# The last rows of a decode kernel's output product, and which engine waits for the output store

## The chip, the cores and the metric

The kernel runs on one core of a Trainium2 chip. The metric is the device time of one execution in microseconds. The core has a matrix engine (TensorE, "PE" in the profile; its weight loads are "PEld"), a vector engine (VectorE, "DVE"), a scalar engine (ScalarE, "ACT"), GpSimd ("POOL") and SyncE ("SP"), which here issues nearly all DMAs. Sixteen DMA engines carry the transfers.

## The reference

One token is decoded. Its normalised vector goes through an attention over a long cache and, beside it, through a small MLP block; all is summed.

```python
xn = layernorm(A_x)                                    # 1 x 1 x 1024
q  = (xn @ wq)                                         # 32 heads of 128
s  = einsum(q, repeat(k_cache, 8)) * 128 ** -0.5       # 4 KV heads x 65536 x 128
o  = einsum(softmax(s), repeat(v_cache, 8)) @ wo       # 4096 x 1024
h  = shift(gelu(layernorm(xn) @ w1)) @ w2              # 1024 x 1024 each
x1 = xn + h
h2 = gelu(layernorm(x1) @ w3) @ w4                     # 1024 x 3584, 3584 x 1024
return A_x + o + x1 + h2                               # bf16
```

All inputs are bf16. The two caches hold 64 MiB (67 MB) each, and each byte is used once.

## The kernel before

The program is written engine by engine. A planner in the file (`_Q`, `_B`, `_op`, `_grp`, `_dma`) keeps one list of operations for each engine and puts a semaphore wait in front of an operation where a buffer it reads or writes is still in use. `q_sp`, `q_pool` and the others are these lists; `wait_all` puts a bare wait at the present end of a list (L37; in the trace such a wait carries line L73).

All loads go through SP's queue in a fixed order: wq, w1, w2, w3, then blocks of 32,768 cache rows of K and V in turn, wo, and at last w4. A large SBUF tile `KV` with three slots takes them. The block loop runs over eight blocks, two for each KV head; TensorE's part of it is a hardware loop. In a block VectorE transposes the K block in place (`Ttr`, L460), TensorE forms scores (`QK`, L474), ScalarE exponentiates, and TensorE multiplies by V (`PV`, L518).

After the last block comes the tail, to which the change belongs:

- `resid_rows` (L598) adds the residual `acc` into one PSUM row for each half of the 1024 outputs, and `wo_rows` (L605) adds the attention's product with wo, 64 matmuls of 512 columns. VectorE (L611) and ScalarE (L612) copy the two rows to SBUF, and four matmuls (L614) put them into bank 0 of the PSUM tile `S_ps` as four rows of 256, on partitions 0, 32, 64 and 96.
- w4 stays as 28 row groups ("rows" below) of 1024 columns; TensorE multiplies row r by column r of `gh_bf`, in four column strips at once. The loads of w4 are cut as `w4_parts` (L569): rows 0 to 16, rows 17 to 23, rows 24 to 26, and row 27 in two halves. They are issued back to back on SP, in front of the end of the last block.
- `out_rows` (L584) takes parts 0 and 1 into bank 0. VectorE copies that bank to SBUF (`ost`, L677).
- `out_halves` (L591) takes rows 24 to 27 in half-width products of 128 columns into banks 2 and 3, one for each half of a strip. For the second half of row 27 `kept_matmul` (L561) uses the weights that TensorE still holds. VectorE adds each bank to its part of `ost` and writes bf16 to `orow` (L682).
- SP issues the store of `orow` (L684) and, as the last instruction of the program, waits for it (L685).

To make the halves, the columns of every strip are ordered as "h j n" (half, strip, column) instead of plainly, in `w4_row`, `resid_rows`, `wo_rows` and in the store.

Of the kernel before, what the change touches and what calls it, by code (L numbers as in the profile page):

```python
# [6 lines left out]
BF = mybir.dt.bfloat16  # L7
F32 = mybir.dt.float32
ACTF = mybir.ActivationFunctionType
ALU = mybir.AluOpType  # L10
# [106 lines left out]
def _op(q, fn, reads=(), writes=(), partial=False, loop=False):  # L117
    _deps(q, reads, writes)
    ev = q.op(fn, True, loop)
    _done(ev, reads, writes, partial)  # L120
    return ev


def _grp(q, fns, reads=(), writes=(), partial=False):
    _deps(q, reads, writes)
    ev = None
    for i, fn in enumerate(fns):
        ev = q.op(fn, i == len(fns) - 1)
    _done(ev, reads, writes, partial)
    return ev  # L130
# [8 lines left out]
def _dma(q, chan, fn, reads=(), writes=(), partial=False):  # L139
    _deps(q, reads, writes)  # L140
    chan.n += 1
    ev = q.dma(fn, chan.sem, 16 * chan.n)
    _done(ev, reads, writes, partial)
    return ev


def bass_parallel_sum__gqa_block_cached__mixer_s_mlp__decode_kernel(
# [13 lines left out]
    P = 128  # L161
    D = A_x.shape[2]
# [6 lines left out]
    KT_F = F // P  # L169
# [9 lines left out]
    with ExitStack() as es:  # L179
        E = es.enter_context  # L180

        def sb(name, shape, dt):
            return E(nc.sbuf_tensor(name, shape, dt))
# [7 lines left out]
        ident_f = sb("ident_f", [P, P], F32)  # L191
# [9 lines left out]
        pT_f = sb("pT_f", [P, 2, 512], F32)  # L201
# [8 lines left out]
        o_bf = sb("o_bf", [P, 32], BF)  # L210
        acc = sb("acc", [P, KT_D], F32)
        gh_bf = sb("gh_bf", [P, KT_F], BF)
# [3 lines left out]
        KV = sb("KV", [P, 3, SLOT], BF)  # L216
# [1 line left out]
        cb_W = sb("cb_W", [P, 4, G, 4], F32)  # L218
        cb_R = sb("cb_R", [P, P], F32)
        cb_o = sb("cb_o", [P, 32], F32)  # L220
        orow = sb("orow", [P, 2, 128], BF)

        e_off = [8 * F]

# [36 lines left out]
        S_ps = ps("S_ps", [P, 4, 512], F32)  # L261
# [12 lines left out]
        def chan(name):  # L274
            if name not in chans:
                chans[name] = _DmaChan(sem("d_" + name))
            return chans[name]
# [14 lines left out]
        def rows_src(w, r0, nrow):  # L292
            return w.rearrange("(p r) n -> p (r n)", p=P)[:, r0 * w.shape[1]:(r0 + nrow) * w.shape[1]]
# [81 lines left out]
        fns = []  # L375
# [173 lines left out]
            _op(q_dve, lambda e: e.reduce_sum(cb_o[0:32, :], cb_R[0:32, :].rearrange("p (a j) -> p j a", j=32), axis=AX.X), reads=[b_cb], writes=[b_cb])  # L549
            _op(q_dve, lambda e: e.tensor_copy(o_bf[32 * h:32 * h + 32, :], cb_o[0:32, :]), reads=[b_cb], writes=[b_o], partial=True)  # L550

        def weights_of(i):
            return (i.tile_position, i.tile_size, str(i.ins[1].memref), i.ins[1].offset, str(i.ins[1].ap))

        def keep_weights(i, name=""):
            r = mybir.InstMatmult(name=name or i.name, engine=i.engine, ins=list(i.ins), outs=list(i.outs), debug=i.debug, start_tensor_calc=i.start_tensor_calc,
                                  stop_tensor_calc=i.stop_tensor_calc, tile_size=i.tile_size, tile_position=i.tile_position,
                                  bass_skip_group_check=i.bass_skip_group_check, ldweights=False)
            return r

        def kept_matmul(e, out_, lhs, rhs, pos):  # L561
            i = e.matmul(out_, lhs, rhs, start=False, stop=True, tile_position=pos, skip_group_check=True).ins
            body = nc.m.functions[0].blocks[-1].instructions
            at = max(k for k, j in enumerate(body) if j.name == i.name)
            assert body[at].opcode == "Matmult" and any(j.opcode == "Matmult" and weights_of(j) == weights_of(i) for j in body[at - 6:at])
            del body[at]
            return e.add_instruction(keep_weights(i, "I-%d" % (1000000 + int(i.name[2:]))))

        w4_parts = [(0, 17 * D), (17 * D, 24 * D), (24 * D, 27 * D), (27 * D, 27 * D + 512), (27 * D + 512, 28 * D)]  # L569
        b_W4 = [_B() for _ in w4_parts]  # L570

        def w4_dma(i):
            c0, c1 = w4_parts[i]
            _dma(q_sp, chan("w4%d" % i), lambda e: e.dma_start(out=KV[:, 2, c0:c1], in_=rows_src(B_w4, 0, KT_F)[:, c0:c1]), writes=[b_W4[i]])

        n_bulk = 2
        b_half = [b_S[2], b_S[3]]
        ost = pT_f[:, 1, 0:256]
        b_ost = b_pT[1]

        def w4_row(r, jj):
            return KV[:, 2, r * D:(r + 1) * D].rearrange("p (h j n) -> p j h n", h=2, j=4)[:, jj, :, :]

        def out_rows(i):  # L584
            c0, c1 = w4_parts[i]
            _grp(q_pe, [lambda e, r=r, jj=jj: e.matmul(
                S_ps[32 * jj:32 * jj + 1, 0, 0:256].rearrange("p (h n) -> p h n", h=2), gh_bf[:, r:r + 1], w4_row(r, jj),
                start=False, stop=(i == n_bulk - 1), tile_position=(0, 32 * jj), skip_group_check=True) for r in range(c0 // D, c1 // D) for jj in range(4)],
                reads=[b_W4[i], b_gh], writes=[b_S[0]], partial=True)

        def out_halves(r, halves, i, first=False, last=False):  # L591
            def mm(e, hf, jj):
                f = kept_matmul if halves == (1,) else lambda e, *a: e.matmul(*a[:3], start=first, stop=last, tile_position=a[3], skip_group_check=True)
                return f(e, S_ps[32 * jj:32 * jj + 1, 2 + hf, 0:128], gh_bf[:, r:r + 1], w4_row(r, jj)[:, hf, :], (0, 32 * jj))
            _grp(q_pe, [lambda e, hf=hf, jj=jj: mm(e, hf, jj) for hf in halves for jj in range(4)],
                 reads=[b_W4[i], b_gh], writes=[b_half[hf] for hf in halves], partial=not first)

        def resid_rows():  # L598
            idc = ident_f[:, :].rearrange("p (h j n) -> p j h n", h=2, j=2)
            _grp(q_pe, [lambda e, j=j, jj=jj: e.matmul(  # L600
                S_ps[32 * jj:32 * jj + 1, 1, :].rearrange("p (h n e) -> p h n e", h=2, e=8)[:, :, :, j], acc[:, j:j + 1], idc[:, jj, :, :],
                start=(j == 0), stop=False, tile_position=(0, 32 * jj), skip_group_check=True) for j in range(KT_D) for jj in range(2)],
                reads=[b_acc, b_const], writes=[b_S[1]])

        def wo_rows():  # L605
            _grp(q_pe, [lambda e, j=j, jj=jj: e.matmul(  # L606
                S_ps[32 * jj:32 * jj + 1, 1, :].rearrange("p (h n) -> p h n", h=2), o_bf[:, j:j + 1],
                KV[:, 0, j * D:(j + 1) * D].rearrange("p (h j n) -> p j h n", h=2, j=2)[:, jj, :, :],
                start=False, stop=(j == 31), tile_position=(0, 32 * jj), skip_group_check=True) for j in range(32) for jj in range(2)],
                reads=b_KV[0] + [b_o], writes=[b_S[1]], partial=True)  # L610
            _op(q_dve, lambda e: e.tensor_copy(pT_f[0:1, 0, :], S_ps[0:1, 1, :]), reads=[b_S[1]], writes=[b_pT[0]])  # L611
            _op(q_act, lambda e: e.activation(pT_f[32:33, 0, :], S_ps[32:33, 1, :], ACTF.Copy), reads=[b_S[1], b_pT[0]], writes=[b_pT[1]])  # L612
            src = pT_f[0:64, 0, :].rearrange("p (h j n) -> p j h n", h=2, j=2)
            _grp(q_pe, [lambda e, jj=jj: e.matmul(  # L614
                S_ps[32 * jj:32 * jj + 1, 0, 0:256].rearrange("p (h n) -> p h n", h=2), ident_f[0:64, 32 * (jj // 2):32 * (jj // 2) + 1], src[:, jj % 2, :, :],
                start=True, stop=False, tile_position=(0, 32 * jj), skip_group_check=True) for jj in range(4)],
                reads=[b_pT[0], b_pT[1], b_const], writes=[b_S[0]])

        def loop_sync(h):
            if h > 0:  # L620
# [51 lines left out]
        _op(q_pool, lambda e: e.memset(pT_f[0:64, 0, :], 0.0), writes=[b_pT[0]])  # L672
        resid_rows()
        wo_rows()
        for i in range(n_bulk):
            out_rows(i)
        _op(q_dve, lambda e: e.tensor_copy(ost, S_ps[:, 0, 0:256]), reads=[b_S[0]], writes=[b_ost])  # L677
        for r in range(24, 27):
            out_halves(r, (0, 1), 2, first=(r == 24))
        for hf in range(2):  # L680
            out_halves(27, (hf,), 3 + hf, last=True)
            _op(q_dve, lambda e, hf=hf: e.tensor_tensor(out=orow[:, hf, :], in0=ost[:, 128 * hf:128 * hf + 128], in1=S_ps[:, 2 + hf, 0:128], op=ALU.add),  # L682
                reads=[b_ost, b_half[hf]], writes=[b_orow], partial=(hf == 1))
        ev_out = _dma(q_sp, chan("out"), lambda e: e.dma_start(out=out[0, 0, :].rearrange("(h j n) -> j h n", h=2, j=4), in_=orow[0:97:32, :, :]), reads=[b_orow])  # L684
        q_sp.wait_all([ev_out])  # L685

        code = nc.m.functions[0].blocks[0].instructions
        heads = {e: next(i for i in code if i.opcode == "Drain" and i.engine == e) for e in (nc.sync.engine, nc.scalar.engine)}
# [51 lines left out]
        for k, i in enumerate(code):  # L740
            if i.opcode != "Matmult":
                continue
            key = weights_of(i)
            if key == prev and i.ins[1].dtype == BF and not i.sync_info:
                code[k] = keep_weights(i)
                n_ld += 1
            prev = key
        assert n_ld > 40, n_ld
# [28 lines left out]
```

## Time and profile before

| What | Value |
|---|---|
| Median of 4 runs | 400.35 us (400.27 to 400.57) |
| The profiled execution's own time | 400.40 us |
| Its span, first to last instruction | 399.1 us |
| Mean granted TensorE clock | 0.645 |
| DMA packets | 3907, 169.97 MB, 426 GB/s over the span |
| Last w4 loads, issue to landing | 28 to 33 us |
| Store of the output | 2.0 KB, issue instruction 0.68 us |

The span begins with the first instruction of the kernel and ends with the last; the time of an execution also holds what the runtime puts around them. Lines of the profile read "line engine operation out<-in shape xcount | busy". An idle time in brackets names what ended it. "SPq" is SP's instruction stream, where DMAs are issued.

### The profile page before, as it was taken

The page shows a single profiled execution, that of the slowest core. Times are in us where ns is not written, and L with a number is a line of the kernel's source. Part 1 is how long each engine was busy: PE and PEld are TensorE (multiplying, and loading weights), DVE is VectorE, ACT ScalarE, POOL GpSimd, SP SyncE. Part 2 cuts the span into 40 slices and gives each one's busy share as a digit, 9 for nine tenths or more (in the row PEclk, how much of TensorE's full clock was granted, in tenths as well). Part 3 has the DMA queues.
Part 4 walks back from the last instruction along what each step waited for, and adds up shares of the span by engine and source line. Part 5 has one row for each costly group of instructions (what it writes and reads, how often), then busy time and mean ns, then how long its engine had stood idle before and what let it go on. Part 6 is the DMA issues. An engine that isn't in the chain of part 4 may idle for free.

```text
span 399.1 us, 3462 instructions
## 1 busy us (share of the span) xinstructions
PE 169.1 (42%) x1539; PEld 59.2 (15%) x1496; DVE 221.9 (56%) x262; ACT 23.9 (6%) x50; POOL 7.6 (2%) x31
## 2 busy tenths in 40 slices
PE   0034767338033713460357036413541362137394
PEld 0011334012001200110012011100120110012232
DVE  0024222994298549834984597269647952895201
ACT  1000000011001100110011002000100110011000
POOL 5000000000000000000000000000000000000000
PEclk9998568555655665575557555855585558555969
DMA  9999899999999999999999999999999999999995
GB/s 421 421 388 493 383 428 466 460 416 427 420 434 422 420 453 466 420 427 420 427 434 420 447 466 427 421 420 427 434 427 447 466 427 420 420 427 434 418 413 231
DMA packets 3907, 169.97 MB, mean 426 GB/s; under 512 B 572, under 2 KB 828, under 8 KB 956
## 3 DMA queue, kind: packets, MB, share of 16 engines
q1 hardware_dynamic: 3756, 169.87, 98.7%
q8 instruction: 5, 0.08, 0.1%
q10 hardware_dynamic: 144, 0.00, 0.0%
q14 instruction: 2, 0.02, 0.0%
HBM read 169.87 MB, written 0.00 MB: 426 GB/s over the span
## 4 chain that ended last, share of the span: by engine, by line
DMA 59%; DVE 25%; PE 13%; issue 1%; ACT 1%; SPq 0%; POOL 0%; DVEq 0%
DMA KV<-in_A_k_cache_dram 45%; DVE KV L460 18%; DMA KV<-in_B_w_dram 8%; DMA KV<-in_A_x_dram 6%; PE S_ps L411 3%; PE OT_ps L518 2%; DVE mrow L481 2%; PE M_ps L426 2%; PE S_ps L474 2%; PE S_ps L379 1%; ACT p_sb L496 1%; DVE Yall L395 1%; DVE pT_f L509 1%; DVE pT_f L419 1%; PE PT_ps L505 0%
## 5 line engine op out<-in xcount | busy, mean ns | idle before, releaser
L460 DVE STREAM_TRANSPOSE KV<-KV 128x4096 f32<-128x4096 f32 x32 | 140.3, 4421 | 44.3 <-DMA KV<-in_A_k_cache_dram 44.3
L474 PE MATMUL S_ps<-KV,Ycur 128*32 128x512 bf16 x512 | 60.7, 624 | 132.5 <-DVE KV L460 132.5
L518 PE MATMUL OT_ps<-KV,pT_f 128*32 128x512 bf16 x512 | 47.3, 512 | 4.0 <-issue 3.1
L474 PEld LDWEIGHTS S_ps<-KV,Ycur 128*32 128x32 bf16 x512 | 14.3, 126 | 159.9 <-DVE KV L460 142.4
L496 ACT ACTIVATE p_sb<-S_ps,brun 128x1024 bf16<-128x1024 f32 x16 | 17.8, 1113 | 276.7 <-DVE brun L494 176.2
L509 DVE STREAM_TRANSPOSE pT_f<-PT_ps 128x512 f32<-128x512 f32 x32 | 22.5, 702 | 14.0 <-PE PT_ps L505 14.0
L481 DVE TENSOR_REDUCE mrow<-S_ps 128x1 f32<-128x1024 f32 x16 | 19.3, 1205 | 11.3 <-PE S_ps L474 11.3
L484 PE MATMUL M_ps<-Rm,Lmat 128*128 128x16 bf16 x16 | 3.1, 194 | 38.0 <-DVE Rm L482 38.0
L529 DVE SCALAR_TENSOR_TENSOR O_acc<-O_acc,ff,OT_ps 128x512 f32<-128x512 f32 x12 | 9.0, 748 | 14.7 <-PE OT_ps L518 14.7
L518 PEld LDWEIGHTS OT_ps<-KV,pT_f 128*32 128x32 bf16 x512 | 13.1, 115 | 23.7 <-issue 16.4
L411 PE MATMUL S_ps<-KV 128*32 128x512 bf16 x88 | 12.1, 538 | 2.7 <-DVE KV L359 2.7
L339 DVE CAST KV<-KV 128x8 f32<-128x8 bf16 x1 | 0.2, 172 | 22.2 <-DMA KV<-in_A_x_dram 22.2
L606 PE MATMUL S_ps<-KV,o_bf 128*1 128x512 bf16 x64 | 9.9, 484 | 4.6 <-DMA KV<-in_A_wo_dram 4.6
L505 PE MATMUL PT_ps<-p_sb,permR 128*128 128x512 bf16 x16 | 9.7, 608 | 0.8
L484 PEld LDWEIGHTS M_ps<-Rm,Lmat 128*128 128x128 bf16 x16 | 1.7, 104 | 49.3 <-DVE Rm L482 49.3
L426 PE MATMUL M_ps<-ident_f,pT_f 64*128 64x2 f32 (+2 forms) x32 | 7.9, 372 | 2.5 <-DVE pT_f L419 2.5
L611 DVE COPY pT_f<-S_ps 1x512 f32<-1x512 f32 x1 | 0.7, 678 | 14.4 <-PE S_ps L606 14.4
L426 PEld LDWEIGHTS M_ps<-ident_f,pT_f 64*128 64x128 f32 (+2 forms) x32 | 7.7, 326 | 4.7 <-DVE pT_f L419 3.1
L419 DVE COPY pT_f<-S_ps 64x512 f32<-64x512 f32 (+1 forms) x3 | 2.1, 686 | 10.8 <-PE S_ps L411 10.8
L505 PEld LDWEIGHTS PT_ps<-p_sb,permR 128*128 128x128 bf16 x32 | 3.3, 103 | 27.5 <-ACT p_sb L496 14.7
L364 PE MATMUL M_ps<-KV 8*128 8x8 bf16 x1 | 0.2, 183 | 16.0 <-DVE Dmat_f L363 16.0
L672 POOL MEMSET pT_f<- 64x512 f32 x1 | 0.5, 519 | 312.4 <-PE OT_ps L518 312.4
(92 smaller groups left out, 90.8 us busy)
## 6 DMA issues: line engine op xcount, KB each, us to landing
KV<-in_B_w_dram SPq DMA_DIRECT2D x1, 7168.0 KB, 47.8
KV<-in_B_w_dram SPq DMA_DIRECT2D x1, 4352.0 KB, 27.4
KV<-in_B_w_dram SPq DMA_DIRECT2D x2, 2048.0 KB, 28.2
KV<-in_B_w_dram SPq DMA_DIRECT2D x1, 1792.0 KB, 31.3
KV<-in_B_w_dram SPq DMA_DIRECT2D x1, 768.0 KB, 32.8
KV<-in_B_w_dram SPq DMA_DIRECT2D x2, 128.0 KB, 32.6
KV<-in_A_k_cache_dram SPq DMA_DIRECT2D x8, 46.7
KV<-in_A_v_cache_dram SPq DMA_DIRECT2D x8, 28.1
```

What stands on the lines that cost most here:

```text
L411: fns.append(lambda e, j=j, k=k, mv=mv: e.matmul(S_ps[32 * (k % 4):32 * (k % 4) + 32, bank + k // 4, :], vec[:, j:j + 1].broadcast_to([P, ...
L419: _op(q_dve, lambda e, b=b, nb=nb: e.tensor_copy(pT_f[0:32 * nb, b, :], S_ps[0:32 * nb, bank + b, :]), reads=[b_S[bank + b]], writes=[b_pT ...
L426: fns.append(lambda e, b=b, nb=nb, c=c: e.matmul(M_ps[:, c0 + 16 * b + c:c0 + 16 * b + 4 * nb:4], pT_f[0:32 * nb, b, c:512:4], ident_f[0:3 ...
L460: _op(q_dve, lambda e: e.transpose(out=KV32[:, s, o:o + 4096], in_=KV32[:, s, o:o + 4096]), reads=[b_KV[s][sub]], writes=[b_KV[s][sub]], l ...
L474: fns.append(lambda e, we=we, cm=cm, mv=mv: e.matmul(S_ps[32 * cm:32 * cm + 32, n % 4, :], Ycur[:, we, :, :].rearrange("p a g -> p (a g)") ...
L481: _op(q_dve, lambda e: e.reduce_max(mrow[:, k:k + 1], S_ps[:, 2 * k:2 * k + 2, :].rearrange("p b c -> p (b c)"), axis=AX.X), reads=b_S[2 * ...
L496: _op(q_act, lambda e: e.activation(p_sb[:, :, :].rearrange("p b c -> p (b c)"), S_ps[:, 2 * k:2 * k + 2, :].rearrange("p b c -> p (b c)") ...
L505: _op(q_pe, lambda e: e.matmul(PT_ps[:, :], permR[:, :], p_sb[:, n % 2, :], start=True, stop=True), reads=[b_p[n % 2], b_const], writes=[b ...
L509: _op(q_dve, lambda e: e.transpose(out=pT_f[:, n % 2, :], in_=PT_ps[:, :]), reads=[b_PT], writes=[b_pT[n % 2]], loop=True)
L518: fns.append(lambda e, q=q, q4=q4: e.matmul(OT_ps[32 * q4:32 * q4 + 32, g % 2, :], pT_bf[:, n % 2, q, :, 1], KV[:, s, 8192 * sub + 512 * q ...
L529: _op(q_dve, lambda e: e.scalar_tensor_tensor(out=O_acc[:, 0:512], in0=O_acc[:, 0:512], scalar=ff[:, k:k + 1], in1=OT_ps[:, k, :], op0=ALU ...
L606: _grp(q_pe, [lambda e, j=j, jj=jj: e.matmul(S_ps[32 * jj:32 * jj + 1, 1, :].rearrange("p (h n) -> p h n", h=2), o_bf[:, j:j + 1], KV[:, 0 ...
```

## The change

It does two things. The last rows of w4 are no longer treated apart: row 27 comes in one DMA, all 28 rows go through `out_rows` into the one bank, and one VectorE copy turns it into `orow`; `ost`, the two banks, the kept weights and the "h j n" order go. And the wait for the output store, which is still issued by SP, stands at the end of GpSimd's list instead of SP's.

```diff
-        orow = sb("orow", [P, 2, 128], BF)
+        orow = sb("orow", [P, 256], BF)
...
-        w4_parts = [(0, 17 * D), (17 * D, 24 * D), (24 * D, 27 * D), (27 * D, 27 * D + 512), (27 * D + 512, 28 * D)]
+        w4_parts = [(0, 17), (17, 7), (24, 3), (27, 1)]
         b_W4 = [_B() for _ in w4_parts]

         def w4_dma(i):
-            c0, c1 = w4_parts[i]
-            _dma(q_sp, chan("w4%d" % i), lambda e: e.dma_start(out=KV[:, 2, c0:c1], in_=rows_src(B_w4, 0, KT_F)[:, c0:c1]), writes=[b_W4[i]])
...
+            r0, nr = w4_parts[i]
+            _dma(q_sp, chan("w4%d" % i), lambda e: e.dma_start(out=KV[:, 2, r0 * D:(r0 + nr) * D], in_=rows_src(B_w4, r0, nr)), writes=[b_W4[i]])
+
+        OUT = S_ps[:, 0, 0:256]
+        b_OUT = b_S[0]
+
+        def out_rows(items, reads, last=False):
+            fns = []
+            for lhs, rhs in items:
+                for jj in range(4):
+                    fns.append(lambda e, lhs=lhs, rhs=rhs, jj=jj: e.matmul(
+                        S_ps[32 * jj:32 * jj + 1, 0, 0:256], lhs, rhs[:, 256 * jj:256 * jj + 256],
+                        start=False, stop=last, tile_position=(0, 32 * jj), skip_group_check=True))
+            _grp(q_pe, fns, reads=reads, writes=[b_OUT], partial=True)
...
-        for i in range(n_bulk):
-            out_rows(i)
-        _op(q_dve, lambda e: e.tensor_copy(ost, S_ps[:, 0, 0:256]), reads=[b_S[0]], writes=[b_ost])
-        for r in range(24, 27):
-            out_halves(r, (0, 1), 2, first=(r == 24))
-        for hf in range(2):
-            out_halves(27, (hf,), 3 + hf, last=True)
-            _op(q_dve, lambda e, hf=hf: e.tensor_tensor(out=orow[:, hf, :], in0=ost[:, 128 * hf:128 * hf + 128], in1=S_ps[:, 2 + hf, 0:128], op=ALU.add),
-                reads=[b_ost, b_half[hf]], writes=[b_orow], partial=(hf == 1))
-        ev_out = _dma(q_sp, chan("out"), lambda e: e.dma_start(out=out[0, 0, :].rearrange("(h j n) -> j h n", h=2, j=4), in_=orow[0:97:32, :, :]), reads=[b_orow])
-        q_sp.wait_all([ev_out])
+        for i, (r0, nr) in enumerate(w4_parts):
+            out_rows([(gh_bf[:, r:r + 1], KV[:, 2, r * D:(r + 1) * D]) for r in range(r0, r0 + nr)], [b_W4[i], b_gh], last=(i == len(w4_parts) - 1))
+        _op(q_dve, lambda e: e.tensor_copy(orow[:, :], OUT), reads=[b_OUT], writes=[b_orow])
+        ev_out = _dma(q_sp, chan("out"), lambda e: e.dma_start(out=out[0, 0, :].rearrange("(j n) -> j n", j=4), in_=orow[0:97:32, :]), reads=[b_orow])
+        q_pool.wait_all([ev_out])
```

In `resid_rows`, `wo_rows` and the four matmuls behind them, operands that were taken in two pieces by the "h" order become contiguous ones of the same size. The number of their instructions stays the same.

## The prediction

> **What bounds the kernel now.** I began with the page: the shares of the engines, the DMA row, and the chain that ended last.
>
> ```profile
> PE 169.1 (42%) x1539; PEld 59.2 (15%) x1496; DVE 221.9 (56%) x262; ACT 23.9 (6%) x50; POOL 7.6 (2%) x31
> DMA  9999899999999999999999999999999999999995
> DMA 59%; DVE 25%; PE 13%; issue 1%; ACT 1%; SPq 0%; POOL 0%; DVEq 0%
> ```
>
> The loads fill the span up to its last slice, and no engine is near full. Up to the landing of the last w4 bytes the time is set by 169.87 MB at 426 GB/s; the edit changes no byte of that. What it can change is the stretch after those bytes, so I asked for the timeline and the chain from 375 us on, and for the waits of SP's queue.
>
> ```profile
> 394.09 0.94 PE L586 MATMUL S_ps<-KV,gh_bf 128*1 128x256 bf16 x28 [0.71 <-DMA KV<-in_B_w_dram]
> 395.08 0.42 DVE L677 COPY pT_f<-S_ps 128x256 f32<-128x256 f32 x1 [4.94 <-PE S_ps L586]
> 395.98 0.58 PE L593 MATMUL S_ps<-KV,gh_bf 128*1 128x128 bf16 x28 [0.95 <-DMA KV<-in_B_w_dram]
> 396.68 0.22 PE L562 MATMUL S_ps<-KV,gh_bf 128*1 128x128 bf16 x4
> 396.68 0.61 DVE L682 TENSOR_TENSOR orow<-pT_f,S_ps 128x128 bf16<-128x128 f32 x2 [1.18 <-PE S_ps L593]
> 397.33 0.68 SPq L684 DMA_DIRECT2D out_dram<-orow  x1
> ```
>
> ```profile
> 396.62 0.02 DVEq L73
> 396.64 0.04 issue
> 396.68 0.30 DVE orow L682
> 396.98 0.03 issue
> 397.01 0.29 DVE orow L682
> ```
>
> ```profile
> SPq L684 <- DVE orow L682: 32.8, 1, 32.8
> SPq L73 <- DMA out_dram<-orow: 1.0, 1, 1.0
> ```
>
> TensorE waits for DMA before part 1 (0.71 us) and before part 2 (0.95 us), so all that precedes, wo_rows included, has slack. The two adds run back to back: the second starts 0.04 us after the first ends, so the split gains only part of an add. The semaphore records of the same trace give the instants. The last of 16 engines reports part 2 at 395.933, half 0 at 396.290, half 1 at 396.633. L562 starts at 396.676 and releases VectorE at 396.918; the second add's result is posted at 397.309. SP issues the store at 397.326 for 0.680; its first packet starts at 398.605, its last landing is 399.022, and SP's wait ends at 399.055, the end of the 399.1 us span. The execution itself took 400.40 us, 1.3 us more, of which the closing handshake of the engines is part; the median of the four runs is 400.35. I add my sum to both.
>
> **The change, part by part.**
>
> Last load. Two DMAs of 128 rows of 1 KB become one of 2 KB rows. On the last engine parts 3 and 4 take 396.633 - 395.933 = 0.700 us for 8 + 8 packets. Packets of 6,144 bytes cost 0.2345 us each on an engine and those of 14,336 bytes 0.5385, so a packet costs some 0.0065 us plus 0.037 us per KB (1,000 bytes); 2,048 bytes give about 0.0825 and eight of them 0.66, with the semaphore 0.67. Gain 0.03, bounds 0.00 and 0.10. One issue fewer on SP (0.43 us) lies 30 us ahead of its landing, behind queued transfers, and is worth nothing; were the queue empty it would be 0.43.
>
> The early rows. The 24 half-width products of part 2 become 12 of 256 columns. A 256-column row of four takes 0.108 us at L586, so three rows from 395.978 end their issue at about 396.30, before the last landing. Nothing, since the wait for the last bytes covers it; uncovered it would be at most 0.33. Removing L677 is likewise free: it lies in 395.08 to 395.50, while PE waits for DMA. The contiguous operands in resid_rows and wo_rows, and L614's, sit ahead of the 0.71 us wait and cost nothing.
>
> Last row on TensorE. Now, landing to released VectorE is 396.918 - 396.633 = 0.285. For four products of 256 columns: 0.043 to start, then from first start to release as in part 1 (last row's four start at 394.742, release at 395.053), 0.311, in all 0.355. Loss 0.07.
>
> VectorE. Now, release to posted result is 397.309 - 396.918 = 0.391: a separate wait instruction, then the second add (0.286). After: one wait on the copy itself (0.024 at L677) and a 128x256 copy out of PSUM, 0.424, posted 0.435 after its start: 0.459. Writing bf16 rather than f32 makes no difference in the rows of 128x512 (691 ns in both). Loss 0.07.
>
> Store. Its issue has two free dimensions now (eight runs of 256 bytes), afterwards four runs of 512. No row shows that form: the loads cost 0.328 after a wait and 0.433 behind another issue, this store 0.680, but a load has 128 rows on 16 engines and the store four on four, which stays so. Bounds: 0 and a gain of 0.35; I take 0.15, nearer to the store's own row, since only one of its two peculiarities goes. First packet minus end of issue is 0.60, unaffected. Each engine then moves one packet instead of two: the second packet starts 0.017 after the first, gain 0.02 (0.00 to 0.04).
>
> The wait. GpSimd has nothing left after the memset at 369.73 and nothing queued behind the wait; SP has nothing behind it either. What changes is the handshake. The trace records nine increments of its semaphore: three in a row at 397.080, 397.114 and 397.153 (as soon as PE is through), one at 397.441 (0.13 after VectorE's last post), then 399.177 (0.12 after SP's wait) and 399.220, 399.258, 399.293, 399.339. I read it as a walk up through PE, two others of which one is GpSimd, VectorE and SP, and down again. SP is its top, so a late SP delays only the way down; a late GpSimd sends the walk up through VectorE and SP first. Where that happens at the very end (400.293, 400.337, 400.360, 400.459 us) the two hops up cost 0.044 and 0.023, and the turn back 0.099 instead of the 0.043 now: 0.12 more (0.16 if GpSimd is second rather than third). GpSimd's own wake-up: its memset started 0.049 after its release, SP's wait 0.016 after the landing: 0.03 more. What it does between the end of its wait and its increment is in no row; I take SP's 0.12, with bounds of 0.00 below and 0.15 above that. Together a loss of 0.15, from 0.00 to 0.34.
>
> The Trainium skill (Runtime: NRT & Kernel Launch, "The ~15µs preamble/postamble breakdown") speaks against the change here: it describes the barrier as a serpentine of eight hops at 44 ns. By that page two extra hops up would cost an estimated 0.09, against the 0.12 of the rows, and the sum would be 0.03 lower. Another page (DMA: Bandwidth & Descriptors, "Specifications") puts 512 B as the least transfer for line rate, smaller ones being read, modified and written; this trace shows 18 ns for a 256-byte packet and cannot show what follows it.
>
> Sum: -0.03 + 0.07 + 0.07 - 0.15 - 0.02 + 0.15 = +0.09 us. Up to the wait's end it is about -0.03, so the span stays near 399.1; the rest falls outside it. On the profiled execution: 400.49; on the median: 400.44. I forecast 400.45. With all bounds: -0.10 + 0.14 - 0.35 - 0.04 = -0.35 below, or 400.0; 0.14 + 0.34 = +0.48 above, or 400.83.
>
> **The rivals.**
>
> A: the store becomes a plain one and the handshake costs nothing. Then -0.03 + 0.14 - 0.35 - 0.02 = -0.26, or 400.1. For it: all loads with one run per row issue in 0.33 to 0.43. Against: the four-engine store is unlike them in more than this. It is still no change that can be told.
>
> B: slower, by one instruction fetch. The DMA records show 16 KB fetches at 377.19 and 394.37, taking 1.07 and 1.11 us of one DMA engine each. Five of the 16 engines end about 1.1 us after the others (396.122 to 396.633 against 394.605 to 395.079); the fetch at 394.37 evidently found an engine whose data were through. PE's program is shorter by 28 instructions (60 become 32 for rows 24 to 27), and other programs by one or two. If a fetch therefore comes to one of the five late engines before its w4 data are through, that is, ahead of 396.1, the last landing moves by its 1.05: 400.35 + 0.09 + 1.05 = 401.5. Against: up to L586 the instructions of PE are the same in number and order, so both fetches should come where they did.
>
> C: GpSimd leaves its wait much later than SP. It decides from 0.75 us of extra delay on; 0.8 of it would give 401.25. Against: its 0.049 start after a release at L672, and its two semaphore instructions at the start take 0.017 each, as SP's does.
>
> D: faster than can be explained by the store, because the late engines are fewer. If all five were as the rest, the last landing would be 396.6 - 1.55 = 395.1, but PE ends part 1 there, so about 1.3 would be gained: 399.1. Nothing in the edit moves the earlier fetches that made these engines late.
>
> **How the numbers follow.** About 0.2%, 0.8 us, is what a measurement of this kernel can tell from no change. Forecast 0.64 and A 0.19 lie within it; B 0.08 and C 0.05 are slower; D 0.04 is faster. So 0.04 faster, 0.83 the same, 0.13 slower. The range takes forecast and A with their bounds and 0.07 of scatter above (the four runs lie in 400.27 to 400.57): 400.0 to 400.9. B, C and D, 0.17 together, lie outside.
>
> **What would show it.** Right: the last w4 landing within 0.1 of 396.6; four products at about 396.65; one copy of 0.42 us on VectorE from about 396.98; the store issued at about 397.43, 0.1 later than now, but shorter than 0.68; the last wait on GpSimd rather than SP, ending near 399.05; time minus span 1.4 to 1.5 instead of 1.3. Wrong: an issue still at 0.68, which takes the 0.15 back; a last landing near 397.7 with one more 16 KB fetch among the w4 packets (B); a GpSimd wait that ends over 0.2 after the store's last landing, or time minus span over 2.0 (C).

## The result

The changed kernel takes 400.98 us (median of 40 runs, 400.80 to 401.25), the kernel before 400.48 us (60 runs, 400.19 to 400.75). The ratio is 1.0013, with a 95% interval of 1.0009 to 1.0018: 0.50 us more. The forecast was 0.09 us more, 400.45, in a range of 400.0 to 400.9; the time lies 0.08 above that range, on the side of the small loss that was forecast. Of the 0.53 between forecast and time, 0.13 is the base: the first four runs of the kernel before had a median of 400.35, sixty have 400.48. From 400.48 the same bounds would have reached 401.03 and held the time. The other 0.4 is a term of the sum.

The profile after has the same frame as before (DMA at nine tenths up to the last slice, 169.97 MB at 426 GB/s), and its span is 399.2 us against 399.1. But the profiled execution took 400.99 us, so 1.8 us now lie outside the span, where there were 1.3. From the timeline of the changed kernel's tail (start, busy time, engine, line; weight loads left out):

```profile
394.06 0.94 PE L566 MATMUL S_ps<-KV,gh_bf 128*1 128x256 bf16 x28 [1.85 <-DMA KV<-in_B_w_dram]
396.13 0.87 PE L566 MATMUL S_ps<-KV,gh_bf 128*1 128x256 bf16 x16 [1.13 <-DMA KV<-in_B_w_dram]
397.05 0.42 DVE L647 CAST orow<-S_ps 128x256 bf16<-128x256 f32 x1 [8.07 <-PE S_ps L566]
397.50 0.63 SPq L648 DMA_DIRECT2D out_dram<-orow  x1
```

And the end of its chain:

```profile
396.08 0.04 issue
396.13 0.90 PE S_ps L566 x16
397.02 0.02 issue
397.05 0.42 DVE orow L647
```

One copy of 0.42 us stands where two adds of 0.30 and 0.29 stood, and the store is issued 0.17 later than before, for 0.63 instead of 0.68. GpSimd's wait for the store ends at 399.197, SP's ended at 399.055. Up to here little has happened. The semaphore records in the traces show the rest. In the closing handshake the engines raise one semaphore in turn; the columns are the end of the wait, then its nine increments, in us:

```
                     wait ends | up: five increments                     | down: four
before   (SP)        399.055   | 397.080 397.114 397.153 397.441 399.177 | 399.220 399.258 399.293 399.339
changed  (GpSimd)    399.197   | 397.186 397.220 399.739 399.783 399.807 | 399.904 399.942 399.978 400.025
```

SP raised the semaphore 0.122 us after its wait; GpSimd needs 0.542. From its increment to the ninth it takes 0.286, from SP's it took 0.162.

### The profile page after: what moved, and what is told of

Read it like the earlier page. It is cut to its first block, busy times and chain, and to the rows that moved or that the text cites. A ratio compares the mean times of both kernels' runs of the same rounds, so it can differ in the third digit from the quotient of the medians.

```text
span 399.2 us, 3429 instructions
## 1 busy us (share of the span) xinstructions
PE 167.4 (42%) x1523; PEld 58.3 (15%) x1484; DVE 221.3 (55%) x260; ACT 23.9 (6%) x50; POOL 7.7 (2%) x31
## 2 busy tenths in 40 slices
DMA packets 3759, 169.97 MB, mean 426 GB/s; under 512 B 548, under 2 KB 552, under 8 KB 808
## 4 chain that ended last, share of the span: by engine, by line
DMA 59%; DVE 25%; PE 13%; issue 1%; ACT 1%; SPq 0%; POOL 0%
DMA KV<-in_A_k_cache_dram 45%; DVE KV L460 17%; DMA KV<-in_B_w_dram 8%; DMA KV<-in_A_x_dram 6%; PE S_ps L411 3%; PE OT_ps L518 2%; DVE mrow L481 2%; PE M_ps L426 2%; PE S_ps L474 2%; PE S_ps L379 1%; ACT p_sb L496 1%; DVE Yall L395 1%; DVE pT_f L509 1%; DVE pT_f L419 1%; PE PT_ps L505 0%
## 5 line engine op out<-in xcount | busy, mean ns | idle before, releaser
L518 PE MATMUL OT_ps<-KV,pT_f 128*32 128x512 bf16 x512 | 46.2, 501 | 3.9 <-issue 2.9
L578 PE MATMUL S_ps<-KV,o_bf 128*1 128x512 bf16 x64 | 8.7, 439 | 4.6 <-DMA KV<-in_A_wo_dram 4.6
```

The lines of the kernel that those rows point to most:

```text
L518: fns.append(lambda e, q=q, q4=q4: e.matmul(OT_ps[32 * q4:32 * q4 + 32, g % 2, :], pT_bf[:, n % 2, q, :, 1], KV[:, s, 8192 * sub + 512 * q ...
L578: _grp(q_pe, [lambda e, j=j, jj=jj: e.matmul(S_ps[32 * jj:32 * jj + 1, 1, :], o_bf[:, j:j + 1], KV[:, 0, j * D + 512 * jj:j * D + 512 * (j ...
```

## The experiments

The yardstick for the wait is the time of a run minus its span: it holds what lies outside the kernel's own instructions. A run's span is recorded to 0.1 us, so single values scatter by that much. The median is 1.29 us for the kernel before in each of the three groups of runs below, and 1.81 for the changed one. For the tail, the span itself and the records serve.

**The two parts apart.**

```diff
 # e1, in the changed kernel
-        q_pool.wait_all([ev_out])
+        q_sp.wait_all([ev_out])
 # e2, in the kernel before
-        q_sp.wait_all([ev_out])
+        q_pool.wait_all([ev_out])
```

> The changed tail, but SP waits for the store again. In the profiled executions the changed kernel ends 0.595 us later than the kernel before. Theory (the wait): GpSimd raises the closing handshake's semaphore 0.54 us after its wait, SP did 0.12 after; with the two hops up (0.12) and a closing part that is 0.09 shorter the wait's place costs 0.46, the tail 0.13. So this kernel is 0.45 faster than the changed one: about 400.55 to 400.6, some 0.1 over the kernel before. Rival (the tail): the last four products ran at half clock and the 256-column copy is long, and the whole 0.5 is from there: about 400.95.

> The tail of the kernel before, in halves, but GpSimd waits for the store. Theory (the wait): 0.46 over the kernel before, about 400.94, and the handshake's third increment again 0.54 us after GpSimd's wait. Rival (the tail): no more than 0.05 over it, about 400.5.

| Kernel | Tail | Waits | Median, us | Beside before (33 runs, 400.55) | Time minus span |
|---|---|---|---|---|---|
| e1 | changed | SP | 400.61 (11 runs) | 1.0002 (0.9993 to 1.0011) | 1.27 |
| e2 | before | GpSimd | 400.97 (11 runs) | 1.0013 (1.0004 to 1.0022) | 1.83 |

The wait does it. In e2's records GpSimd's wait ends at 399.320 and its increment comes at 399.863, 0.543 later. The changed tail alone is 0.06 over the kernel before, within what these runs can tell. The closing part that I had taken 0.09 shorter with GpSimd's wait is no effect of it: the stretch from the ninth increment to the next one is 0.79 in e1, where SP waits, as in the changed kernel and in e2, but 0.88 in the kernel before and in e4 below; why is open. It need not belong to the kernel: over the runs of the changed kernel alone, time minus span goes from 1.75 to 1.93, which is more than the rounding of the span makes.

**Whose wait.**

```diff
 # e3, in the changed kernel; e5 with q_pe, e6 with q_dve
-        q_pool.wait_all([ev_out])
+        q_act.wait_all([ev_out])
```

> The changed tail, ScalarE waits for the store. ScalarE is second in the handshake, one hop before GpSimd. Theory (GpSimd itself is slow to leave): ScalarE leaves in about 0.12 to 0.15 and pays three hops up instead of two, 0.16, less 0.09 at the close: 0.1 to 0.2 over the same tail with SP's wait. Rival (every engine but SP is slow to leave a wait): 0.54 to leave, so at or 0.04 over the changed kernel, about 401.0.

> The changed tail, TensorE waits for the store. So far time minus span is 1.29 us where SP waits, 1.83 where GpSimd does, 1.67 where ScalarE does. TensorE is first in the handshake. Theory (hops, plus a leaving time of each engine's own): four hops up, 0.14, and the turn back 0.05 longer give 0.20 with a leaving time like SP's 0.12, so 1.49; ScalarE's remaining 0.22 is then its own. Rival (what ScalarE and GpSimd pay is paid by any engine that sits below VectorE in the order): 1.7 to 1.85.

> The changed tail, VectorE waits for the store. It is one hop below SP. Theory: hop of 0.024 and turn back 0.054 longer, leaving time about as SP's: 0.08 over SP's 1.29, so 1.37. Rival (any engine but SP pays 0.2 to 0.4 of its own): 1.6 or more.

| Kernel | Waits | Leaves after, us | First increment of its own to ninth | Time minus span | Median; beside before |
|---|---|---|---|---|---|
| e5 | TensorE | 0.196 | 0.358 | 1.53 | 400.81; 1.0008 (0.9999 to 1.0017) |
| e3 | ScalarE | 0.119 | 0.324 | 1.67 | 400.95; 1.0012 (1.0003 to 1.0021) |
| changed | GpSimd | 0.542 | 0.286 | 1.81 | 400.98; 1.0013 (1.0009 to 1.0018) |
| e6 | VectorE | 0.146 | 0.242 | 1.39 | 400.57; 1.0003 (0.9994 to 1.0013) |
| e1 | SP | 0.121 | 0.163 | 1.27 | 400.61; 1.0002 (0.9993 to 1.0011) |

The third and fourth columns are of one profiled execution each. The order of the walk is thereby shown: TensorE, ScalarE, GpSimd, VectorE, SP, and back. With TensorE's wait all nine increments come after it, with ScalarE's all but one, with GpSimd's all but two, with VectorE's all but three, with SP's all but four. The lower an engine stands in it, the dearer its late arrival, from 0.16 to 0.36. The page "Runtime: NRT & Kernel Launch" of the Trainium skill ("The ~15µs preamble/postamble breakdown") gives some 355 ns for such a walk, in its row on the barrier ahead of a kernel. The closing one takes 0.358 us in e5, where nothing of it is hidden. GpSimd alone has a long way out. TensorE's and VectorE's cases came within 0.05 of the theory's 1.49 and 1.37. ScalarE's did not: 1.45 was due by the records, 1.67 was measured, and 0.22 of it is in none of them. That became a question of its own (e10).

**Is it the waiting or the leaving?**

```diff
 # e4, in the changed kernel
-        _op(q_dve, lambda e: e.tensor_copy(orow[:, :], OUT), reads=[b_OUT], writes=[b_orow])
+        ev_cp = _op(q_dve, lambda e: e.tensor_copy(orow[:, :], OUT), reads=[b_OUT], writes=[b_orow])
...
-        q_pool.wait_all([ev_out])
+        q_pool.wait_all([ev_cp])
+        q_sp.wait_all([ev_out])
 # e7, in e1, in the loop over w4_parts; ev_pe is the end of the part's products
...
+            if i == 1:
+                q_pool.wait_all([ev_pe])
+                for _ in range(6):
+                    _op(q_pool, lambda e: e.memset(O_acc[:, 0:512], 0.0), writes=[b_Oacc])
```

> The changed tail; SP waits for the store, and GpSimd waits only for VectorE's last copy, some 1.7 us earlier. Theory (a fixed delay in which GpSimd leaves its program): the handshake's third increment comes 0.54 us after GpSimd's wait, at about 398.05, long before SP's, and the time is that of the changed tail with SP's wait. Rival (the delay comes from waiting for a DMA, or from being last): the increment comes 0.12 after the wait, at about 397.6; the time is the same.

> The changed tail with SP's wait; GpSimd, instead of sleeping from 370 us on, is woken at the end of part 1 (about 395 us), runs six memsets of 128x512 on a tile that nothing reads any more, and ends its program with the last of them, without a bare wait, at about 398.1. Theory (GpSimd's way out of the program takes 0.54 whatever came before): its increment comes 0.5 to 0.6 after the last memset's end. Rival (the delay is that of waking from a bare wait or from a long sleep): about 0.12 after it.

In e4 GpSimd's wait for VectorE's copy ends at 397.766, and its increment comes at 398.309: 0.543 again, though it waits for no DMA and is not the last. The time is 400.57 (1.0001, 0.9992 to 1.0010), with 1.31 outside the span: off the path the same delay costs nothing. In e7 GpSimd's line in the timeline reads

```profile
395.20 3.44 POOL L650 MEMSET O_acc<- 128x512 f32 x6 [24.82 <-PE S_ps L566]
```

The last memset starts at 398.118 and takes 0.524, to 398.642; the increment comes at 399.171, 0.529 later. The time of this one run is 400.60. So it is neither the wake-up from a bare wait nor a long sleep. GpSimd takes 0.53 to 0.54 us from the last thing in its program to its place in the handshake. What it does in that time the traces do not show.

**A better tail, tried.** In e8 (SP waits) row 27 comes in one DMA, all products are 128 columns wide with the two halves of a strip in banks 0 and 2 (the four products in front of part 0 too, which become eight), and the last copies run side by side.

```diff
 # e8, in e1
...
-                for jj in range(4):
...
+                for h in range(2):
+                    for jj in range(4):
...
+                            S_ps[32 * jj:32 * jj + 1, 2 * h, 0:128], lhs, rhs[:, 256 * jj + 128 * h:256 * jj + 128 * h + 128],
...
+        _op(q_dve, lambda e: e.tensor_copy(orow[:, 0:128], S_ps[:, 0, 0:128]), reads=[b_OUT], writes=[b_orow])
+        _op(q_act, lambda e: e.activation(orow[:, 128:256], S_ps[:, 2, 0:128], ACTF.Copy), reads=[b_OUT2], writes=[b_orow2])
...
```

> SP waits. Row 27 in one DMA; all products of the output row are 128 columns wide, each strip's halves in a bank of their own, and in the end VectorE copies one bank and ScalarE the other at the same time. Landing to first half 0.285 and second 0.34, then a 128-column copy of 0.30 (VectorE) or 0.2 (ScalarE): posted 0.61 us after the last landing, against 0.68 in the kernel before and 0.81 in the changed one; with the store's 0.05 and the load's 0.05 about 0.15 below the kernel before, 400.4. Rival (instruction fetches): TensorE has some 220 instructions more in the tail, about one 16 KB fetch; if it comes to one of the five late DMA engines ahead of its w4 data, the last landing is 1.05 later: 401.4.

It took 401.40 us beside 400.49 (1.0023, 1.0014 to 1.0032): the rival's number, but not its mechanism. The last w4 landing is at 396.524, the earliest of all twelve traces. From the timeline of e8:

```profile
394.06 0.45 PE L568 MATMUL S_ps<-KV,gh_bf 128*1 128x128 bf16 x20 [1.79 <-DMA KV<-in_B_w_dram]
396.35 1.56 PE L568 MATMUL S_ps<-KV,gh_bf 128*1 128x128 bf16 x68 [1.84 <-issue]
397.84 0.29 DVE L653 CAST orow<-S_ps 128x128 bf16<-128x128 f32 x1 [8.86 <-PE S_ps L568]
397.94 0.28 ACT L655 ACTIVATE orow<-S_ps 128x128 bf16<-128x128 f32 x1 [8.35 <-PE S_ps L568]
```

TensorE stops for 1.84 us in the midst of part 1, whose data have landed, and the profile names no releaser but "issue". The two copies do run side by side, in 0.29 and 0.28, but 68 products now start at 396.35, and most of them run after the last landing. To tell whether the banks or the length of the program had stopped it, e9 adds instructions alone:

```diff
 # e9, in e1, behind part 0
+            if i == 0:
+                _grp(q_pe, [lambda e, k=k: e.matmul(S_ps[32 * (k % 4):32 * (k % 4) + 1, 3, 0:32], gh_bf[:, k % 28:k % 28 + 1], KV[:, 2, 32 * k:32 * k + 32],
+                    start=True, stop=True, tile_position=(0, 32 * (k % 4)), skip_group_check=True) for k in range(80)], reads=[b_W4[0], b_gh], writes=[b_S[3]])
```

> The changed tail with SP's wait, and 80 small extra products (32 columns each, into a bank that nobody reads) after part 0, where TensorE waits for part 1 anyway: 160 TensorE instructions more, as the kernel with two banks had 220 more and stopped for 1.84 us with 'issue' in the midst of part 1, after 546 recorded TensorE instructions behind the loop. Theory (TensorE runs out of fetched instructions at that point): the same stop, at some 30 to 40 instructions into part 1, until about 396.3; the rest then lies behind the last landing, so the time is 0 to 0.4 over that of the changed tail with SP's wait. Rival (it was the two banks or ScalarE): part 1 runs through in 0.95 us as ever.

From the timeline of e9:

```profile
392.47 0.82 PE L648 MATMUL S_ps<-KV,gh_bf 128*1 128x32 bf16 x80
394.48 0.61 PE L566 MATMUL S_ps<-KV,gh_bf 128*1 128x256 bf16 x16 [1.20 <-DMA KV<-in_B_w_dram]
396.48 0.94 PE L566 MATMUL S_ps<-KV,gh_bf 128*1 128x256 bf16 x28 [1.39 <-issue]
```

The stop is there, after 16 products of part 1 with their weight loads, 32 instructions, as forecast; the one run took 400.87. In both traces TensorE stops after the same number of recorded instructions, 473 from the first product with wo on. So the stop goes with the place in TensorE's program, not with the banks or with ScalarE. In both a 16 KB instruction fetch begins before it (393.73 in e8, 394.12 in e9). That the stop waits for this fetch fits, but nothing ties the two directly, and the other ten traces have a fetch between 393.6 and 394.4 too and no stop. Counted the same way, the kernel before ends 76 instructions ahead of that place, the changed one 104. No version here is clearly faster than the kernel before.

**ScalarE's 0.22.**

```diff
 # e10, in e1, behind L583
+            _op(q_act, lambda e: e.activation(O_acc[32:33, 0:64], S_ps[32:33, 1, 0:64], ACTF.Copy), reads=[b_S[1]], writes=[b_Oacc])
```

> The changed tail with SP's wait; ScalarE runs one small activation more at about 389.6, seven us ahead of the end, whose result nobody reads. Two kernels had an instruction more on ScalarE, and both took 0.22 us that no semaphore record shows. Theory (it is ScalarE's program that is longer, not its wait): time minus span 1.5 instead of 1.29. Rival (it is ScalarE being busy or waiting close to the end): 1.29, as with SP's wait.

Time minus span is 1.50 in the median, between 1.46 and 1.55 in ten runs; the kernel before, beside it, has 1.21 to 1.40. One small instruction more on ScalarE, seven us ahead of the end, costs 0.2 us outside the span, as in e3 and e8. The median is 400.66 beside 400.43 (1.0004, 0.9995 to 1.0014).

The records tell where it is not. In e3, e8 and e10 the profiled execution's own time is 0.05 us longer than the stretch from the first instruction to the last recorded increment of the handshake's semaphore; in the kernel before, the changed one, e1, e2, e4, e5, e6 and e9 it is 0.18 shorter. So the 0.23 lies outside that stretch, ahead of it or behind it. It may not be ScalarE's alone: in e7, where GpSimd has six instructions more, the same difference is 0.04 shorter, so that 0.14 is added (one run). Whether it is the number of instructions or where they fall in memory is open.

## Why the prediction was wrong

The step that failed is the last of the wait's: "What it does between the end of its wait and its increment is in no row; I take SP's 0.12, with bounds of 0.00 below and 0.15 above that." It measured 0.54, that is 0.42 above SP's. Put into the sum, 0.09 + 0.42 = 0.51, against 0.50 measured. That the two agree so closely is luck: with the store's issue as it was measured the sum is 0.6, and the interval of the measured difference goes from 0.36 to 0.72. The value was the nearest row, but the upper bound of 0.15 came from none. The arguments against rival C were rows of GpSimd starting work and of short semaphore instructions; they tell of waking, and the delay is in leaving. C's mechanism, a late leaving, was the right one, at 0.42 of extra delay. That lies between the 0.15 that the range allowed and the 0.75 from which C was to decide, and there was no case for what lies between.

The other terms, by the profiles:

| Term | Forecast | Measured |
|---|---|---|
| Last load as one DMA, last engine | -0.03 | -0.05 (last landing of part 2 to the end: 0.700 before, 0.640 to 0.654 in eight traces with the changed loads); -0.2 in the changed kernel's profile (0.487) and in e6 (0.508) |
| Last row on TensorE | +0.07 | +0.07 in e1 (0.353 from landing to release); +0.17 in the changed kernel's profile |
| VectorE | +0.07 | +0.07 (0.459 from release to post) |
| Store's issue | -0.15 | -0.05 (0.633 for 0.680; 0.625 in the later groups of runs) |
| Store's packets | -0.02 | +0.01 (end of issue to last landing 1.023 for 1.016) |
| GpSimd's wake-up | +0.03 | +0.01 |
| Hops | +0.12 | +0.12 |
| GpSimd's leaving | 0.00 | +0.42 |

The store's issue is the second mis-sized term: four runs on four engines still cost nearly what eight did. So the extra dimension made 0.05 of the 0.35 by which the issue was longer than a load's (0.680 for 0.328). TensorE's larger loss in the changed kernel's profile is the granted clock. The same stretch of e1 and then of the changed kernel, with busy times by engine, clock, DMA share and GB/s:

```profile
396.60:397.20 0.60, 0.40 (x11) 0.09 (x4) 0.00 (x0) 0.00 (x0) 0.00 (x0) 1.00 0.00 0
```

```profile
396.60:397.20 0.60, 0.40 (x8) 0.09 (x4) 0.15 (x1) 0.00 (x0) 0.00 (x0) 0.50 0.00 0
```

At half clock the last four products took 0.37 instead of 0.27. The clock fell at 396.53 in that execution, but at 398.14, 397.82 and 399.03 in e1, e3 and e4, which have the same tail, and at 398.90 in the kernel before. So it is the phase of one execution and no part of the change.

Right were the reading that everything ahead of the last landing has cover, the walk of the handshake and the price of its hops, and that both instruction fetches come about where they did (377.28 and 393.90, for 377.19 and 394.37) and delay no landing, so that rival B did not come. Rival A's plain store did not come either, and D's late engines are still late. The sign was right, and the loss is below what 0.2% would tell; but sixty and forty runs told it.

## What to carry to other kernels

Here the last wait belongs on the engine that stands at the turn of the closing handshake and leaves fast, which is SP. VectorE comes close (0.1 us more), and GpSimd costs half a microsecond, which no instruction in the profile shows. Compare time minus span, not spans alone, whenever the end of a program is edited. Where a cost is in no row, a fraction of another engine's cost is no bound for it; one run with the wait alone moved, as e2, measures it.

## What the runs showed of the hardware

- GpSimd takes 0.53 to 0.54 us from the end of its program to the closing handshake in all four traces where it could be seen (changed, e2, e4 and e7); the other engines took 0.12 to 0.20.
- TensorE stopped 1.84 us (e8) and 1.39 us (e9, one run) for "issue" at the same place of its straight code behind the loop, 473 recorded instructions from the first product with wo on. The ten traces whose programs end before that place show no such stop in the tail.
- One activation more on ScalarE cost 0.2 us outside the span (e10: time minus span 1.50 for 1.27 in e1), without an event in the records.
